# Another statically searched order of the same 3061 operations for a two-layer banded-attention and MLP kernel, with other engine choices for some of them

## The chip, the cores and the metric

The kernel runs on one core of a Trainium2 chip. A core has TensorE (PE in the profile, its weight loads PEld), VectorE (DVE), ScalarE (ACT), GpSimd (POOL) and SyncE (SP), which only issues transfers here. The metric is the device time of one execution in microseconds (us), as the median of the runs. A run more than 1.5% above the fastest of its kernel counts as slow, the others as fast.

## The reference, cut to what matters

```python
x = A_x                                                 # 2048 x 512, bf16
x = x + _A_ref(_layernorm(x), A_wqkv, A_wo)             # attention: 32 heads of 16, window of 256 back
x = x + _B_ref(_layernorm(x), B_w1, B_b1, B_w2, B_b2)   # MLP 512 -> 1792 -> 512, tanh GELU
x = x + _A_ref(_layernorm(x), A_wqkv, A_wo)             # the same weights a second time
x = x + _B_ref(_layernorm(x), B_w1, B_b1, B_w2, B_b2)
```

## The kernel before

The kernel first describes its work as nodes (engine, function, a nominal duration, what is read and written, PSUM banks taken and freed). Then three lists, found offline by a search, decide everything: `_ORDER` is the order in which nodes are put into the five engine queues, `_ALT` names the nodes that run on their second engine, and `_BANKS` is the PSUM bank of each allocation.

```python
for i in _ALT:                                  # second engine instead of the first
    nodes[i]["eng"], nodes[i]["fn"], nodes[i]["dur"] = nodes[i]["alts"][1][:3]
...
for i in _ORDER:
    ...                                         # asserts dependencies, takes and frees banks
return _ORDER
...
for i in order:                                 # an engine runs its own nodes strictly in this order
    nd = PL.nodes[i]
    S_.op(nd["eng"], ..., reads=phys(nd["reads"]), writes=phys(nd["writes"]), dma=nd["dma"])
```

Each engine works its queue in order and waits on semaphores for the others, so a node that is placed too early in a queue holds up everything behind it.

The unit of attention is a score visit: 512 score columns for four row groups on TensorE (`sc`), then two exponentials of 128x1024 on ScalarE, then one or two 0/1 masks, each on VectorE or GpSimd:

```python
add("pe", sc, 250.0, reads=rd, writes=["ps:" + gA, "ps:" + gB], ...)
for gi, g_ in enumerate((gA, gB)):
    add("act", ...activation(E[...], ps[...], AF.Exp, scale=SCALE)...)
for k, (n, off, cnt) in enumerate((HEADM if head else FULLM)[v]):
    n1 = cnt * w / 128.0
    add("dve", ...tensor_tensor(out=Ew, in0=Ew, in1=Mw, op=ALU.mult)..., 140.0 + 275.0 * n1,
        ..., alt=(("pool", ...same..., 100.0 + 1052.0 * n1, POOL_H, True),))
```

There are 150 visits and so 300 exponentials. Other nodes with two possible engines are the copies of Q and V out of PSUM (VectorE or ScalarE), the normalisation of the attention output and a small layernorm addition (both VectorE or GpSimd). The edited numbers 250, 140, 275, 100 and 1052 are nominal: no instruction that is issued depends on them.

The softmax here doesn't subtract the row's maximum and nothing guards it: scores larger than these inputs give would overflow.

Of the kernel before, what the change touches and what calls it, by code (L numbers as in the profile page):

```python
# [7 lines left out]
ALU = mybir.AluOpType  # L8
# [11 lines left out]
class _Sched:  # L20
# [148 lines left out]
    14, 7, 33, 8, 15, 34, 9, 16, 13, 35, 17, 36, 18, 4, 37, 0, 19, 10, 38, 1, 20, 2, 39, 45, 21, 3, 40, 22, 43, 23,  # L169
    41, 24, 25, 44, 42, 46, 91, 26, 47, 27, 28, 48, 89, 29, 30, 31, 52, 32, 92, 49, 90, 50, 93, 53, 94, 51, 11, 98,  # L170
    54, 99, 5, 6, 65, 95, 66, 67, 60, 61, 62, 63, 82, 96, 68, 97, 83, 84, 85, 144, 55, 56, 86, 57, 100, 58, 64, 69,
    111, 112, 75, 76, 77, 59, 113, 114, 78, 142, 162, 116, 143, 164, 145, 117, 115, 118, 146, 119, 147, 163, 12,
    148, 167, 120, 169, 70, 71, 72, 73, 215, 168, 106, 107, 149, 217, 108, 101, 79, 102, 150, 170, 103, 104, 216,
    74, 151, 121, 109, 122, 123, 124, 105, 128, 88, 125, 129, 130, 166, 131, 218, 110, 81, 219, 171, 132, 220, 172,
    221, 134, 245, 223, 173, 133, 181, 157, 224, 158, 183, 246, 175, 174, 247, 165, 182, 185, 222, 248, 187, 184,
    152, 153, 87, 154, 155, 249, 159, 135, 156, 252, 186, 253, 126, 160, 235, 254, 127, 161, 255, 188, 189, 236,
    237, 256, 80, 225, 238, 259, 138, 226, 258, 261, 227, 228, 136, 140, 137, 229, 260, 250, 263, 239, 141, 264,
    262, 176, 265, 267, 177, 268, 190, 266, 269, 271, 191, 273, 240, 192, 178, 272, 193, 275, 179, 241, 242, 277,
    274, 276, 284, 270, 243, 194, 286, 278, 230, 180, 231, 285, 244, 232, 288, 233, 287, 289, 195, 234, 196, 197,
    290, 198, 331, 292, 200, 199, 294, 201, 202, 203, 329, 349, 350, 293, 204, 300, 351, 291, 352, 483, 302, 353,  # L180
    301, 296, 295, 279, 298, 205, 297, 207, 373, 208, 206, 375, 209, 536, 210, 330, 537, 303, 374, 377, 211, 379,
    538, 212, 376, 280, 378, 381, 467, 539, 383, 281, 385, 299, 380, 387, 304, 332, 282, 333, 382, 213, 334, 283,
    386, 214, 384, 540, 389, 305, 257, 388, 359, 390, 360, 361, 306, 391, 335, 354, 307, 336, 355, 362, 308, 398,
    363, 366, 392, 251, 356, 400, 357, 367, 364, 358, 368, 369, 399, 314, 365, 315, 316, 317, 337, 370, 499, 318,
    309, 500, 371, 310, 311, 321, 804, 312, 338, 501, 313, 402, 322, 319, 393, 403, 502, 320, 652, 404, 653, 503,
    394, 505, 409, 410, 323, 339, 405, 340, 504, 507, 650, 341, 342, 509, 411, 416, 506, 417, 343, 556, 557, 508,
    558, 651, 418, 559, 541, 580, 401, 413, 788, 581, 414, 510, 582, 324, 654, 511, 583, 560, 415, 584, 512, 561,
    585, 562, 327, 563, 586, 564, 328, 588, 565, 406, 590, 407, 587, 420, 372, 344, 421, 408, 589, 422, 592, 325,
    345, 594, 346, 347, 655, 566, 567, 395, 326, 593, 348, 596, 568, 396, 569, 598, 423, 424, 139, 425, 597, 605,
    591, 573, 574, 544, 606, 595, 570, 607, 609, 542, 572, 575, 599, 576, 611, 437, 543, 438, 513, 439, 440, 397,  # L190
    427, 452, 514, 428, 429, 610, 453, 454, 577, 455, 442, 545, 462, 443, 444, 445, 515, 441, 463, 430, 612, 464,
    465, 600, 608, 466, 457, 516, 446, 517, 426, 518, 519, 458, 456, 459, 520, 521, 432, 412, 433, 434, 435, 601,
    447, 431, 460, 448, 449, 461, 436, 546, 526, 450, 547, 548, 451, 613, 527, 602, 419, 549, 603, 522, 615, 550,
    523, 524, 670, 525, 671, 672, 673, 528, 529, 614, 674, 617, 530, 531, 551, 552, 618, 553, 604, 484, 616, 619,
    621, 485, 532, 486, 623, 533, 487, 620, 554, 873, 488, 489, 622, 534, 694, 555, 490, 535, 491, 695, 492, 624,
    493, 494, 495, 696, 496, 698, 497, 700, 625, 498, 656, 699, 658, 657, 468, 626, 469, 701, 702, 470, 659, 704,
    471, 627, 703, 578, 472, 706, 628, 571, 727, 707, 473, 579, 474, 1011, 629, 475, 476, 708, 477, 478, 728, 479,
    729, 480, 719, 709, 481, 720, 660, 482, 730, 665, 731, 721, 820, 666, 732, 667, 741, 875, 668, 742, 710, 743,
    737, 711, 669, 661, 662, 738, 712, 663, 630, 664, 631, 632, 633, 713, 723, 634, 783, 725, 734, 640, 735, 635,
    636, 724, 876, 722, 637, 784, 638, 785, 786, 874, 639, 726, 758, 759, 787, 760, 761, 642, 744, 748, 749, 641,  # L200
    750, 736, 675, 751, 643, 745, 739, 762, 644, 768, 769, 697, 645, 770, 740, 771, 705, 676, 677, 678, 772, 778,
    779, 752, 780, 781, 877, 746, 763, 878, 764, 765, 646, 747, 753, 754, 755, 679, 766, 647, 680, 756, 767, 773,
    774, 757, 775, 776, 648, 681, 714, 1096, 777, 649, 782, 1098, 733, 836, 715, 687, 837, 688, 689, 682, 683, 716,
    789, 790, 684, 717, 690, 791, 691, 792, 685, 793, 794, 838, 1097, 795, 1099, 881, 693, 840, 1100, 879, 796,
    1101, 718, 842, 797, 880, 798, 799, 839, 800, 841, 801, 844, 882, 802, 898, 845, 803, 899, 900, 901, 692, 846,
    843, 902, 917, 686, 919, 847, 921, 923, 848, 918, 805, 922, 806, 920, 807, 808, 849, 809, 810, 811, 812, 925,
    850, 813, 851, 926, 883, 884, 885, 814, 924, 852, 927, 886, 929, 815, 887, 816, 931, 817, 818, 853, 819, 854,
    930, 855, 933, 856, 934, 888, 932, 857, 889, 890, 891, 935, 1116, 892, 942, 1117, 928, 944, 1118, 1119, 821,
    863, 822, 943, 823, 936, 824, 946, 825, 1120, 947, 937, 948, 858, 938, 859, 1059, 949, 860, 1060, 861, 826, 862,
    827, 828, 1061, 829, 864, 1063, 865, 893, 945, 894, 1065, 895, 896, 830, 897, 831, 1064, 1067, 832, 833, 1069,  # L210
    834, 1062, 1066, 903, 904, 835, 905, 1068, 906, 1140, 939, 1121, 907, 1142, 1122, 1123, 1070, 1124, 910, 911,
    1141, 866, 912, 867, 1125, 1144, 868, 913, 1145, 1071, 940, 914, 1146, 869, 915, 1143, 1148, 1072, 870, 957,
    1149, 958, 953, 871, 1150, 916, 1152, 954, 872, 1154, 1133, 1151, 955, 1134, 1135, 959, 1136, 1153, 960, 1073,
    961, 1137, 1156, 962, 1126, 1158, 1127, 1074, 1128, 1129, 950, 1157, 1130, 951, 1027, 1165, 952, 1132, 967,
    1167, 1104, 968, 1348, 1131, 981, 982, 969, 983, 1166, 984, 909, 1169, 1075, 996, 1105, 1155, 997, 1171, 1212,
    998, 999, 1006, 1007, 941, 1008, 1009, 1170, 991, 992, 1168, 993, 964, 1102, 994, 1210, 1172, 1103, 986, 987,
    995, 988, 1147, 965, 989, 976, 977, 1138, 1081, 1082, 1083, 908, 978, 1010, 1084, 979, 1076, 990, 1077, 966,
    1078, 963, 1079, 1213, 1159, 1001, 971, 1106, 980, 1107, 1080, 1108, 985, 972, 1109, 1085, 1002, 1000, 1003,
    1004, 1211, 973, 1086, 974, 1005, 1160, 956, 1087, 1110, 1088, 970, 1173, 1214, 1028, 1089, 975, 1161, 1090,
    1029, 1030, 1175, 1091, 1031, 1032, 1111, 1215, 1094, 1112, 1113, 1114, 1033, 1092, 1034, 1035, 1115, 1093,  # L220
    1036, 1174, 1037, 1177, 1038, 1039, 1179, 1095, 1176, 1012, 1013, 1040, 1041, 1178, 1014, 1042, 1181, 1015,
    1183, 1162, 1016, 1180, 1235, 1163, 1236, 1237, 1182, 1238, 1254, 1239, 1017, 1018, 1256, 1019, 1020, 1021,
    1216, 1022, 1255, 1184, 1023, 1258, 1433, 1024, 1260, 1025, 1185, 1434, 1026, 1259, 1218, 1364, 1164, 1219,
    1262, 1044, 1186, 1264, 1045, 1046, 1257, 1047, 1139, 1048, 1263, 1435, 1049, 1050, 1217, 1266, 1436, 1187,
    1051, 1268, 1052, 1188, 1053, 1054, 1055, 1267, 1301, 1043, 1270, 1189, 1302, 1272, 1269, 1056, 1304, 1057,
    1265, 1271, 1220, 1221, 1222, 1058, 1223, 1305, 1224, 1279, 1561, 1290, 1281, 1291, 1190, 1261, 1292, 1191,
    1280, 1192, 1193, 1303, 1313, 1314, 1315, 1306, 1316, 1283, 1194, 1323, 1284, 1324, 1437, 1297, 1273, 1200,
# [202 lines left out]
def bass_interleave_layers__sliding_block__dense_activation_gelu__prompt_kernel(  # L430
# [53 lines left out]
    ACT_H, POOL_H, DVE_H = 300.0, 60.0, 0.0  # L484
# [12 lines left out]
    with ExitStack() as kctx:  # L497
        S_ = _Sched(nc, kctx)

        def sb(name, shape, dtype=dt.bfloat16):  # L500
# [36 lines left out]
        add = PL.add  # L537
# [5 lines left out]
            reads=["ident"], writes=["ident"], prio=-200)  # L543
        add("pool", lambda e, B: e.affine_select(
            ident[:], ident[:], [[1, P]], ALU.is_ge, 0.0, base=0, channel_multiplier=-1), 300,
            reads=["ident"], writes=["ident"], prio=-200)
# [8 lines left out]
        for i, conds in enumerate((((1, HK, -1), (0, -HK, 1)), ((1, 0, -1),))):  # L555
            for st, base, cm in conds:
                add("pool", lambda e, B, i=i, st=st, base=base, cm=cm: e.affine_select(
                    mask01[:, i, :], mask01[:, i, :], [[st, HK]], ALU.is_ge, 0.0, base=base, channel_multiplier=cm), 250,
                    reads=["mask01"], writes=["mask01"], prio=50)
# [439 lines left out]
```

## Time and profile before

| | kernel before |
|---|---|
| time, median | 473.71 us when the prediction was made; 473.48 of 4 runs beside the changed kernel |
| span of the profiled run | 468.9 us |
| busy: TensorE, ScalarE, VectorE, GpSimd | 434.1, 388.6, 346.6, 203.5 us |
| first exponential starts, 64th ends | 15.47 us, 87.5 us |
| 300th exponential ends | 426.3 us |

The useful way to read this profile is by stage. The exponentials are good milestones, since every visit has two, both kernels have 300 of them in the same order of blocks, and ScalarE runs them in one line of the timeline. Between the 64th and the 65th ScalarE changes to GELU for the first time. The prediction shows the lines; the stretches after the first milestone are cut slightly differently here. The view is busy time by stretch (length, then each engine's busy us with its instructions in brackets, then TensorE's granted clock, 1.00 being full speed), for the kernel before:

```profile
15.40:54.10 38.70, 28.62 (x577) 16.96 (x573) 32.42 (x56) 32.43 (x38) 13.48 (x13) 0.91 0.30 81
54.10:87.50 33.40, 28.04 (x682) 18.11 (x683) 31.84 (x58) 31.00 (x36) 18.93 (x18) 0.90 0.32 79
87.50:148.60 61.10, 56.35 (x1139) 32.95 (x1136) 45.60 (x80) 54.02 (x66) 25.07 (x20) 1.00 0.19 41
148.60:426.30 277.70, 268.94 (x4827) 149.32 (x4826) 216.37 (x367) 252.81 (x299) 132.20 (x110) 1.00 0.16 32
```

They are exponentials 1 to 32, 33 to 64, 65 to 104 and 105 to 300. In the first two VectorE and ScalarE are both busy most of the time, and TensorE's granted clock is 0.91 and 0.90 instead of 1.

### The profile page before, as it was taken

Reading aid. Unit: us, or ns where it says so; the run is one execution under the profiler, and the core shown is the slowest. Engines: PE = TensorE matmul, PEld = TensorE weight load, DVE = VectorE, ACT = ScalarE, POOL = GpSimd, SP = SyncE. Lnnn points to the kernel's source line nnn. Section 1 sums busy time; section 2 is a strip of 40 time slices with the busy share of each in tenths; the row PEclk is TensorE's granted clock in tenths of the full one; section 3 lists DMA queues with packets and bytes.
Section 4 is the critical chain, followed back from the end, with each engine's and each line's share of the span. In section 5 each row is a group of like instructions: output and inputs, shape, how many; then the busy total and the mean of one; then the engine's idle time right before and its main releaser. Section 6 shows DMA issues by size and latency. Waiting matters only on the chain.

```text
span 468.9 us, 16891 instructions
## 1 busy us (share of the span) xinstructions
PE 434.1 (93%) x7627; PEld 245.0 (52%) x7627; DVE 346.6 (74%) x599; ACT 388.6 (83%) x469; POOL 203.5 (43%) x189
## 2 busy tenths in 40 slices
PE   8877698788989989999999999989999999899997
PEld 4543455544645545565556455545555544545453
DVE  4968999886867996758998786898857769933311
ACT  1588998997989889988899899889989989985441
POOL 4233447315455454644761166534349441434020
PEclk9997889999999999999999999999999999999999
DMA  8551031711120122101221201203020012020122
GB/s 247 202 133 53 15 68 24 194 29 39 25 48 4 36 51 29 31 2 31 43 59 35 51 1 30 45 14 66 1 59 19 3 27 62 3 58 1 30 73 67
DMA packets 47940, 23.51 MB, mean 50 GB/s; under 512 B 34172, under 2 KB 47356, under 8 KB 47868
## 3 DMA queue, kind: packets, MB, share of 16 engines
q1 hardware_dynamic: 47868, 22.43, 20.2%
q8 instruction: 60, 0.98, 0.9%
q14 instruction: 12, 0.10, 0.1%
HBM read 8.00 MB, written 2.10 MB: 22 GB/s over the span
## 4 chain that ended last, share of the span: by engine, by line
PE 74%; ACT 12%; DVE 10%; issue 2%; DMA 1%; POOL 0%; DVEq 0%; SPq 0%
PE ps L665 57%; ACT E L786 11%; PE ps L823 8%; PE ps L779 8%; DVE xn L635 2%; DVE KT L710 2%; DVE stat L612 1%; DVE E L795 1%; DMA X<-in_A_x_dram 1%; DMA xnTA<-xn 1%; DVE X L921 1%; DVE OD L833 1%; DVE QT L600 0%; DVE gT L897 0%; POOL rstd L622 0%
## 5 line engine op out<-in xcount | busy, mean ns | idle before, releaser
L786 ACT ACTIVATE E<-ps 128x1024 bf16<-128x1024 f32 x300 | 284.1, 1038 | 34.6 <-PE ps L779 33.8
L798 POOL TENSOR_TENSOR E<-E,mask 128x1024 bf16<-128x1024 bf16 (+3 forms) x65 | 109.9, 1697 | 89.3 <-ACT E L786 89.0
L665 PE MATMUL ps<-xnTB,W_sb 128*128 128x384 bf16 (+1 forms) x616 | 115.1, 322 | 4.6 <-issue 2.9
L665 PE MATMUL ps<-W_sb,gT 128*128 128x512 bf16 x448 | 112.2, 380 | 2.3 <-issue 2.3
L665 PEld LDWEIGHTS ps<-xnTB,W_sb 128*128 128x128 bf16 x616 | 57.1, 98 | 45.6 <-issue 5.2
L665 PE MATMUL ps<-xnTA,Wqkv_sb 128*128 128x256 bf16 x512 | 73.5, 278 | 3.2 <-DVE X L921 1.8
L779 PE MATMUL ps<-QT,KT 32*128 32x256 bf16 (+3 forms) x1920 | 62.1, 235 | 13.1 <-ACT E L786 7.4
L909 ACT ACTIVATE gT<-ps,b1T 128x384 bf16<-128x384 f32 (+1 forms) x100 | 50.7, 578 | 22.4 <-PE ps L665 22.2
L795 DVE TENSOR_TENSOR E<-E,mask 128x1024 bf16<-128x1024 bf16 (+3 forms) x91 | 61.0, 681 | 11.2 <-ACT E L786 10.9
L665 PEld LDWEIGHTS ps<-W_sb,gT 128*128 128x128 bf16 x448 | 40.4, 98 | 48.1 <-issue 8.0
L779 PEld LDWEIGHTS ps<-QT,KT 32*128 32x128 bf16 x1920 | 32.8, 93 | 60.9 <-ACT E L786 36.1
L665 PEld LDWEIGHTS ps<-xnTA,Wqkv_sb 128*128 128x128 bf16 x512 | 47.6, 99 | 22.0 <-issue 3.0
L841 POOL TENSOR_TENSOR Nb<-OD,Rc 128x512 bf16<-128x512 f32 x24 | 26.0, 1084 | 67.7 <-DVE Rc L837 67.7
L833 DVE STREAM_TRANSPOSE OD<-ps 128x1024 f32<-128x1024 f32 x32 | 39.8, 1244 | 20.4 <-PE ps L823 20.3
L917 POOL TENSOR_TENSOR Xb<-X,b2all 128x512 f32<-128x512 bf16 x32 | 38.0, 1194 | 29.6 <-DVE X L921 22.7
L823 PE MATMUL ps<-E,Va 64*17 64x64 bf16 (+3 forms) x1920 | 45.0, 234 | 3.6 <-ACT E L786 1.5
L921 DVE TENSOR_TENSOR X<-Xb,ps 128x512 bf16<-128x512 f32 x32 | 21.6, 683 | 34.7 <-PE ps L665 34.6
L823 PE MATMUL ps<-E,Vs 64*17 64x64 bf16 (+3 forms) x1920 | 45.4, 234 | 1.7 <-issue 1.7
L823 PEld LDWEIGHTS ps<-E,Va 64*17 64x17 bf16 x1920 | 39.2, 86 | 12.3 <-issue 8.0
L612 DVE BATCH_NORM_STATS2 stat<-X 128x6 f32<-128x512 bf16 x64 | 43.0, 682 | 3.0 <-DMA X<-in_A_x_dram 2.4
L897 DVE TENSOR_SCALAR gT<-ps,b1T 128x384 bf16<-128x384 f32 (+1 forms) x54 | 31.4, 591 | 13.2 <-PE ps L665 12.8
L710 DVE TENSOR_TENSOR KT<-ps,parmask 128x1024 bf16<-128x1024 f32 x32 | 38.7, 1210 | 3.3 <-PE ps L665 3.1
(49 smaller groups left out, 380.1 us busy)
## 6 DMA issues: line engine op xcount, KB each, us to landing
Vs<-Va SPq DMA_DIRECT2D x64, 68.0 KB, 2.1
W_sb<-in_B_w_dram SPq DMA_DIRECT2D x2, 1792.0 KB, 9.6
out_dram<-X SPq DMA_DIRECT2D x16, 128.0 KB, 1.8
X<-in_A_x_dram SPq DMA_DIRECT2D x3, 512.0 KB, 6.2
Wqkv_sb<-in_A_wqkv_dram SPq DMA_DIRECT2D x4, 256.0 KB, 5.2
X<-in_A_x_dram SPq DMA_DIRECT2D x2, 256.0 KB, 3.0
Wqkv_sb<-in_A_wqkv_dram SPq DMA_DIRECT2D x1, 512.0 KB, 6.3
Wo_sb<-in_A_wo_dram SPq DMA_DIRECT2D x1, 512.0 KB, 7.3
```

Of the source, the lines that this page charges most:

```text
L612: add("dve", lambda e, B, t=t, k6=k6: e.bn_stats(stat6[:, k6, :], X[:, t, :]), 680, reads=["X%d" % t], writes=["st%d" % k6], prio=prio[j], ...
L665: r = e.matmul(ps[:, B[g][0], cols], lhsT, rhs, start=st, stop=sp)
L710: add("dve", lambda e, B, g=g, i=i: e.tensor_tensor(out=KT[:, kb, 2 * i : 2 * i + 2, :, :].rearrange("p c m (a n) -> p (c m) a n", a=2), i ...
L779: x = e.matmul(ps[:, bk[r], o : o + n], KT[rows, kb, c, m, :], QT[rows, c, q : q + n], start=True, stop=True)
L786: add("act", lambda e, B, g_=g_, gi=gi: e.activation(E[:, 2 * gi : 2 * gi + 2, e0 : e0 + 512], ps[:, B[g_][0] : B[g_][0] + 2, :], AF.Exp, ...
L795: add("dve", lambda e, B, Ew=Ew, Mw=Mw: e.tensor_tensor(out=Ew, in0=Ew, in1=Mw, op=ALU.mult), 140.0 + 275.0 * n1, reads=["E%d_%d%s" % (sl, ...
L798: alt=(("pool", lambda e, B, Ew=Ew, Mw=Mw: e.tensor_tensor(out=Ew, in0=Ew, in1=Mw, op=ALU.mult), 100.0 + 1052.0 * n1, POOL_H, True),))
L823: x = e.matmul(ps[32 * r : 32 * r + VW, B[g][par], o * HK : (o + q_hi - q_lo) * HK], V[rows, (2 * b + m // 2) % VR, c * HC + 2 * r + par, ...
L833: add("dve", lambda e, B: e.transpose(OD[:, s, :], ps[:, B[g][0] : B[g][0] + 2, :]), 1245, reads=["ps:" + g], writes=["OD%d" % s], prio=pr ...
L897: add("dve", lambda e, B, g=g, fc=fc: e.tensor_scalar(out=gT[:, fc, 0:M], in0=ps[:, B[g][0], 0:M], scalar1=b1T[:, fc : fc + 1], scalar2=No ...
L909: add("act", lambda e, B, g=g, fc=fc: e.activation(gT[:, fc, 0:M], ps[:, B[g][0], 0:M], AF.Gelu_apprx_tanh, bias=b1T[:, fc : fc + 1], scal ...
L917: add("pool", lambda e, B, t=tau % T, xs=xs: e.tensor_tensor(out=Xb[:, xs, :], in0=X[:, t, :], in1=b2all[:], op=ALU.add), 1180, reads=["X% ...
```

## The change

The intent: the search that had found the three lists was continued, with other durations for the masks and the score visits. Apart from the three lists only nominal durations differ:

```diff
 _ORDER = [
-    14, 7, 33, 8, 15, 34, 9, 16, 13, 35, 17, 36, 18, 4, 37, 0, 19, 10, 38, 1, 20, 2, 39, 45, 21, 3, 40, 22, 43, 23,
+    14, 4, 33, 3, 13, 5, 15, 34, 16, 35, 0, 17, 36, 1, 18, 37, 2, 19, 7, 38, 20, 39, 21, 45, 40, 22, 23, 41, 43, 24,
  ... (all of _ORDER, _ALT and _BANKS is replaced)
-                add("pe", sc, 250.0, reads=rd,
+                add("pe", sc, 235.0, reads=rd,
  ...
-                    add("dve", ...tensor_tensor..., 140.0 + 275.0 * n1,
+                    add("dve", ...tensor_tensor..., 145.0 + 270.0 * n1,
  ...
-                        alt=(("pool", ...tensor_tensor..., 100.0 + 1052.0 * n1, POOL_H, True),))
+                        alt=(("pool", ...tensor_tensor..., 182.0 + 970.0 * n1, POOL_H, True),))
```

## The prediction

> **What bounds the kernel now.** I read the page first (shares and slices), then busy time in seven stretches that I cut at events of ScalarE's timeline, then the groups by shape, then the waits.
>
> ```profile
> PE 434.1 (93%) x7627; PEld 245.0 (52%) x7627; DVE 346.6 (74%) x599; ACT 388.6 (83%) x469; POOL 203.5 (43%) x189
> ...
> PE   8877698788989989999999999989999999899997
> ...
> DVE  4968999886867996758998786898857769933311
> ACT  1588998997989889988899899889989989985441
> ```
>
> TensorE looks like the bound (93%), but the slices say that the bound changes: up to slice 9 TensorE is at 6 to 8 tenths while VectorE and ScalarE stand at 8 or 9. So I cut the span at 15.4 us (first exponential starts), 44.9 us (ScalarE becomes dense), 87.5 us (64th exponential done, first GELU), 426.3 us (last exponential done).
>
> ```profile
> core 0: us, PE busy (x) PEld busy (x) DVE busy (x) ACT busy (x) POOL busy (x), PEclk, DMA share, GB/s
> 0.00:15.40 15.40, 13.47 (x87) 7.47 (x88) 9.02 (x22) 2.97 (x4) 4.74 (x19) 1.00 0.89 282
> 15.40:44.90 29.50, 22.13 (x369) 13.22 (x365) 23.39 (x37) 23.23 (x28) 10.02 (x10) 0.88 0.39 105
> 44.90:87.50 42.60, 34.53 (x892) 21.84 (x891) 40.87 (x77) 40.20 (x45) 22.39 (x22) 0.92 0.25 63
> 87.50:180.00 92.50, 85.30 (x1660) 48.86 (x1658) 73.89 (x127) 81.01 (x99) 41.57 (x34) 1.00 0.18 39
> 180.00:300.00 120.00, 119.82 (x2085) 67.73 (x2084) 94.73 (x164) 109.94 (x132) 59.17 (x52) 1.00 0.19 34
> 300.00:426.30 126.30, 120.16 (x2224) 65.67 (x2222) 93.34 (x156) 115.89 (x136) 56.53 (x45) 1.00 0.13 29
> 426.30:468.90 42.60, 38.70 (x326) 20.16 (x324) 11.31 (x19) 15.41 (x30) 9.09 (x10) 0.99 0.16 47
> ```
>
> Columns: length of the stretch, then each engine's busy us with instructions in brackets. Four regimes. (1) To 15.4 us: loads and the first layernorm. (2) 15.4 to 87.5: VectorE 64.3 of 72.1 us and ScalarE 63.4 of 72.1 are the bound together, TensorE has 15.4 us of holes. (3) 87.5 to 426.3: TensorE 325.3 of 338.8, 13.5 us of holes; ScalarE has 32.0 us of holes. (4) The last 42.6 us: MLP matmuls only.
>
> In regime 2 the holes of ScalarE lie at its start:
>
> ```profile
> 15.47 3.84 ACT L786 ACTIVATE E<-ps 128x1024 bf16<-128x1024 f32 x4 [1.88 <-PE ps L779]
> ...
> 23.87 4.69 ACT L786 ACTIVATE E<-ps 128x1024 bf16<-128x1024 f32 x5 [1.48 <-PE ps L779]
> ...
> 31.58 5.61 ACT L786 ACTIVATE E<-ps 128x1024 bf16<-128x1024 f32 x6 [1.12 <-PE ps L779]
> 39.05 5.61 ACT L786 ACTIVATE E<-ps 128x1024 bf16<-128x1024 f32 x6 [1.86 <-PE ps L779]
> ```
>
> (Start, length, instructions, idle time before.) Only 21 exponentials start in the first 29.4 us; with the few copies between them ScalarE is idle for about 6.3 us (29.5 minus 23.2). It waits for scores, and those wait for the VectorE copies and masked K tiles (1.21 us each) that feed them.
>
> **What the Trainium skill says.** "Perfetto Trace Analysis", section Identifying the Most-Contended Engine: matmul busy share is not a good measure of the distance to the limit because matmuls are pipelined. The trace agrees: a W2 matmul is shown with 380 ns, but 36 of them in a row took 7.93 us, 220 ns each. So "TensorE 100% busy" in regime 3 can hide bubbles and I don't take it as a floor. "SBUF — State Buffer", section Who interferes with whom: a VectorE instruction with two SBUF inputs and a GpSimd instruction that reads SBUF exclude each other, the later one fully blocks. The trace agrees: VectorE masks have a median of 675 ns but a longest of 2101 ns, about one GpSimd mask. "ScalarE: Activation LUTs", section What ACT_TABLE_LOAD costs: about 1283 ns for the load itself; here every one took 1283 ns, so switches matter if the new order has more of them.
>
> **The change part by part.** The program's 3061 operations, shapes and dependencies are the same. The four edited duration numbers never reach the chip; what does is the order of the queues, the choice of engine for some operations, and the PSUM banks. I counted each engine's queue in both kernels. Durations:
>
> ```profile
> L798 POOL TENSOR_TENSOR E<-E,mask 128x1024 bf16<-128x1024 bf16 x34 | 72.8, 2141 | 59.4 <-ACT E L786 59.3
> ...
> L795 DVE TENSOR_TENSOR E<-E,mask 128x1024 bf16<-128x1024 bf16 x50 | 37.9, 760 | 6.1 <-ACT E L786 6.1
> ```
>
> *ScalarE*: PSUM copies go from 22 to 14 (7 V copies and 1 Q copy go to VectorE) at some 0.61 us: 4.9 us less. Table loads: 19 switches in both, nothing. *VectorE*: +8 copies at 0.68 = +5.4; normalisations of the attention output 8 to 11 at 0.92 = +2.8; masks 91 to 81 (1 fewer of 256 columns at 0.26, 7 fewer of 512 at 0.58, 2 fewer of 1024 at 0.76) = -5.8. Sum +2.4 us, which is nothing where it has over 100 us of holes. *GpSimd*: 10 masks more (0.8 + 7 x 1.21 + 2 x 2.14 = 13.5), 3 normalisations fewer (-3.3): about +10 us on an engine at 43%. *TensorE*: the same matmuls; changes between row-tiled, column-tiled and full matmuls go from 325 to 330, nothing.
>
> So the total work doesn't decide; what lies in which regime does.
> *Regime 1.* In the new order TensorE has 8.2 us of matmul work ahead of the first score visit instead of 10.1 (256-column matmuls at 109 ns, 512 at 220): the four V matmuls that stood ahead of it now come after it. VectorE's first K tile comes before the second pair of tiles is normalised, in the old order after it and after a bn_stats of 0.69. My estimate: the first exponential at about 13.4 us instead of 15.5, 2 us earlier.
> *Regime 2.* VectorE's queue up to the 64th exponential: 6 masks fewer (4 x 0.76 + 0.58 + 0.26 = -3.9), 2 normalisations fewer (-1.8), one Q copy, one layernorm piece and three small ones fewer (-2.4), 4 V copies more (+2.7): 5.4 us less of a co-bound engine. ScalarE: 2 copies fewer, -1.2 us. GpSimd takes the 6 masks (+10.6 us with 4 long ones) where it has 39.7 us of holes. The ceiling of the gain is the 2 us plus ScalarE's holes, about 6.3 + 1.2; I expect regime 2 to end some 3.5 us earlier in all, since the slower GpSimd masks delay some attention products, and work moved out of the head (4 bias additions, a layernorm piece) comes back later.
> *Regime 3.* About 3.7 us less ScalarE work, but on the engine with 32 us of holes while TensorE is the bound; of the 13.5 us of holes of TensorE the better placing may close a little: 1 us.
> *Regime 4.* After the last score visit 112 W1 pieces, 8 output-projection matmuls and 90 W2 matmuls remain, against 112, 8 and 92: 2 x 0.22 = 0.4 us, taken as none because those two must run earlier.
> Sum: 3.5 + 1 = 4.5 us, 473.7 - 4.5 = 469.2.
>
> **Rivals.** (a) The head gains and nothing arrives: regime 3 is bound by TensorE and by its own chain, and starts when the first layer's last block is normalised, not at the 64th exponential. For it: TensorE's 100% from 180 to 300. Against it: a dense TensorE queue that starts earlier also ends earlier. It would give 472 to 474. (b) GpSimd's masks become the wait: each takes 2.14 us against 0.76, and 10 us more of it locks VectorE more often; the old order shows VectorE masks waiting up to 2.1 us. For it: the search counts a short VectorE mask at 415 ns, where the trace has 583, so it knows nothing of the lock. Against it: no row of the waits has TensorE waiting for a GpSimd mask. It would give 474 to 478. (c) The new order also closes most holes of ScalarE in the head and bubbles hidden inside TensorE's busy time, because it was searched with 235 ns for a score visit instead of 250. It would give 462 to 466. For it: 15.4 us of TensorE holes in regime 2. Against it: the orders of regime 3 look alike; TensorE work ahead of the 100th, 200th and 300th exponential differs by under 1 us.
>
> **Range and chances.** Executions of one kernel spread by 0.3%, 1.5 us; the head's gain I hold to 0 to 7 us, and regime 3 may go either way by 3 us. 80% range 464 to 473.5. Over 2% faster means under 464.2: rival (c), 0.11. Over 2% slower means over 483.2, for which nothing in the counts speaks: 0.01. Within 2%: 0.88.
>
> **What would show it.** First exponential near 13.4 us and the 64th done near 84 (was 87.5); VectorE's busy time until then about 5 us lower; ScalarE's total near 384; last exponential near 422, and from there again some 42.6 us. If the 64th exponential is early and the last one isn't, (a) holds. If VectorE masks take longer and TensorE's attention products wait for GpSimd, (b). If regime 3 shrinks by over 4 us, (c), and my belief that its order is as good as before was wrong.

## The result, and the profile after

The changed kernel takes 458.65 us (457.91 to 460.46, 4 runs), the kernel before 473.48 us (472.66 to 474.78, 4 runs). The ratio is 0.969, with a 95% interval of 0.9654 to 0.9726. Ratios are the mean time of one kernel's fast runs over that of the other's of the same rounds, so not quite the ratio of the medians quoted. The change is 3.1% faster; 469.2 was predicted, with a range down to 464.0. The gain is over three times the predicted one.

The page of the kernel after, its busy shares and slices:

```profile
PE 422.5 (93%) x7565; PEld 241.6 (53%) x7627; DVE 340.8 (75%) x600; ACT 385.4 (84%) x461; POOL 212.2 (47%) x196
...
PE   8986789989999999999989999998999998899997
...
DVE  6978899868878888977987669887666896725311
ACT  2899999989899998888788898998999899976250
```

The totals tell little: the shares are the same as before within a few per cent of the span. The slices tell where: ScalarE stands at 9 in slices 3 to 8, where the kernel before had 8, 8, 9, 9, 8, 9. Busy time by stretch, kernel after, cut at the same milestones (first exponential starts; 32nd, 64th, 104th and 300th ends):

```profile
0.00:12.50 12.50, 10.54 (x76) 6.38 (x78) 8.13 (x20) 3.08 (x4) 4.94 (x19) 1.00 0.86 255
12.50:44.90 32.40, 26.32 (x517) 16.30 (x522) 28.20 (x49) 31.67 (x36) 23.01 (x20) 1.00 0.58 171
44.90:78.10 33.20, 28.35 (x743) 17.81 (x747) 29.90 (x56) 30.61 (x34) 14.74 (x15) 0.95 0.31 60
78.10:135.30 57.20, 53.80 (x1125) 32.49 (x1133) 45.09 (x80) 53.75 (x66) 29.97 (x26) 1.00 0.18 33
135.30:412.80 277.50, 264.12 (x4783) 148.35 (x4824) 215.29 (x374) 250.53 (x294) 134.26 (x111) 1.00 0.18 32
412.80:456.20 43.40, 39.32 (x326) 20.32 (x326) 14.14 (x25) 15.82 (x29) 5.28 (x5) 0.99 0.15 43
```

Stage by stage, after minus before, in us:

| stage | before | after | difference |
|---|---|---|---|
| until the first exponential | 15.4 | 12.5 | -2.9 |
| exponentials 1 to 64 | 72.1 | 65.6 | -6.5 |
| exponentials 65 to 104 | 61.1 | 57.2 | -3.9 |
| exponentials 105 to 300 | 277.7 | 277.5 | -0.2 |
| after the last exponential | 42.6 | 43.4 | +0.8 |
| span | 468.9 | 456.2 | -12.7 |

These are one trace each; the medians differ by 14.8 us. So, as far as these traces go, the whole gain lies in the first third, and the 196 exponentials after it take the same time in both. In the second row ScalarE's busy time fell by 1.1 us only (63.43 to 62.28); its holes, length less busy time, fell from 8.7 to 3.3 us. The timeline of ScalarE in the new kernel (start, length, instructions, idle time before) shows it:

```profile
12.53 1.94 ACT L786 ACTIVATE E<-ps 128x1024 bf16<-128x1024 f32 x2 [0.64 <-PE ps L779]
...
15.14 1.94 ACT L786 ACTIVATE E<-ps 128x1024 bf16<-128x1024 f32 x2 [0.17 <-PE ps L779]
...
21.01 23.94 ACT L786 ACTIVATE E<-ps 128x1024 bf16<-128x1024 f32 x26 [0.34 <-PE ps L779]
```

The prediction shows four gaps of 1.1 to 1.9 us up to 39 us in the kernel before; here 26 exponentials run as one piece from 21.0 to 44.9 us, and at 45 us 32 are done instead of 22.

VectorE's groups by shape explain a part. The first two lines are of the kernel before until its 64th exponential, the next two of the kernel after until its own (busy us and mean ns of one, then idle time before):

```profile
L635 DVE TENSOR_SCALAR xn<-X,statmv,rstd 128x512 bf16<-128x512 bf16 x16 | 8.0, 504 | 1.4 <-POOL rstd L622 1.2
L795 DVE TENSOR_TENSOR E<-E,mask 128x512 bf16<-128x512 bf16 x7 | 4.1, 592 | 1.4 <-ACT E L786 1.4
```

```profile
L635 DVE TENSOR_SCALAR xn<-X,statmv,rstd 128x512 bf16<-128x512 bf16 x15 | 6.0, 418 | 0.4 <-DMA xnTB<-xn 0.2
L795 DVE TENSOR_TENSOR E<-E,mask 128x512 bf16<-128x512 bf16 x6 | 2.4, 419 | 0.0
```

The same instructions are shorter on average: a mask of 512 columns takes 419 ns instead of 592, a layernorm normalisation 418 instead of 504. With 6 to 16 of a kind, these means hang on a few long ones. Of the seven masks before, five took 413 to 427 ns, one 671 and one 1377. One normalisation took four times its usual time, while GpSimd was doing a mask of its own (19.40 to 21.04 us):

```profile
19.53 1.65 DVE L635 TENSOR_SCALAR xn<-X,statmv,rstd 128x512 bf16<-128x512 bf16 x1
```

VectorE masks of over 1 us number eleven in the kernel before, two of them in this stretch, and seven in the kernel after, none of them in this stretch; every one started while a GpSimd instruction was running. Over the whole kernel the masks did not all become shorter: 512 columns went from 583 to 513 ns, 1024 columns from 760 to 780. In this stretch GpSimd has more masks than before (it is busy for 42.7 us against 37.2), yet VectorE is held up less. VectorE's busy time until the 64th exponential is 66.2 us instead of 73.3.

### The profile page after: what moved, and what is told of

It is laid out like the page before. It is cut to its first block, busy times and chain, and to the rows that moved or that the text cites.

```text
span 456.2 us, 16825 instructions
## 1 busy us (share of the span) xinstructions
PE 422.5 (93%) x7565; PEld 241.6 (53%) x7627; DVE 340.8 (75%) x600; ACT 385.4 (84%) x461; POOL 212.2 (47%) x196
## 4 chain that ended last, share of the span: by engine, by line
PE 69%; ACT 21%; DVE 6%; issue 3%; DMA 2%; SPq 0%; DVEq 0%
PE ps L665 51%; ACT E L786 16%; PE ps L779 8%; PE ps L823 8%; ACT gT L909 2%; DVE OD L833 1%; PE ps L570 1%; ACT gT L900 1%; DVE E L795 1%; DMA xnTA<-xn 1%; DMA xnTB<-xn 1%; DVE gT L897 1%; DVE xn L635 1%; ACT L786 1%; ACT L909 1%
## 5 line engine op out<-in xcount | busy, mean ns | idle before, releaser
L786 ACT ACTIVATE E<-ps 128x1024 bf16<-128x1024 f32 x300 | 284.1, 1040 | 27.8 <-PE ps L779 27.1
L798 POOL TENSOR_TENSOR E<-E,mask 128x1024 bf16<-128x1024 bf16 (+3 forms) x75 | 122.7, 1648 | 82.1 <-ACT E L786 81.9
L665 PE MATMUL ps<-xnTB,W_sb 128*128 128x384 bf16 (+1 forms) x616 | 113.3, 322 | 5.1 <-DVE X L921 1.2
L665 PE MATMUL ps<-W_sb,gT 128*128 128x512 bf16 x418 | 108.7, 380 | 3.1 <-issue 2.1
L665 PE MATMUL ps<-xnTA,Wqkv_sb 128*128 128x256 bf16 x512 | 72.1, 274 | 3.2 <-ACT E L786 1.0
L779 PE MATMUL ps<-QT,KT 32*128 32x256 bf16 (+3 forms) x1920 | 61.4, 232 | 9.8 <-ACT E L786 6.2
L909 ACT ACTIVATE gT<-ps,b1T 128x384 bf16<-128x384 f32 (+1 forms) x100 | 51.2, 574 | 21.6 <-PE ps L665 21.3
L779 PEld LDWEIGHTS ps<-QT,KT 32*128 32x128 bf16 x1920 | 32.3, 93 | 56.7 <-ACT E L786 29.9
L795 DVE TENSOR_TENSOR E<-E,mask 128x1024 bf16<-128x1024 bf16 (+2 forms) x81 | 53.3, 670 | 10.0 <-ACT E L786 9.9
L823 PE MATMUL ps<-E,Vs 64*17 64x64 bf16 (+3 forms) x1920 | 44.4, 231 | 1.9 <-issue 1.9
L823 PE MATMUL ps<-E,Va 64*17 64x64 bf16 (+3 forms) x1920 | 44.0, 231 | 2.0 <-issue 1.0
L622 POOL TENSOR_TENSOR rstd<-rstd,mhalf 128x2 f32<-128x2 f32 x32 | 23.5, 734 | 34.5 <-DVE rstd L618 33.0
## 6 DMA issues: line engine op xcount, KB each, us to landing
W_sb<-in_B_w_dram SPq DMA_DIRECT2D x2, 1792.0 KB, 11.7
```

The source lines that it names most:

```text
L665: r = e.matmul(ps[:, B[g][0], cols], lhsT, rhs, start=st, stop=sp)
L779: x = e.matmul(ps[:, bk[r], o : o + n], KT[rows, kb, c, m, :], QT[rows, c, q : q + n], start=True, stop=True)
L786: add("act", lambda e, B, g_=g_, gi=gi: e.activation(E[:, 2 * gi : 2 * gi + 2, e0 : e0 + 512], ps[:, B[g_][0] : B[g_][0] + 2, :], AF.Exp, ...
L795: add("dve", lambda e, B, Ew=Ew, Mw=Mw: e.tensor_tensor(out=Ew, in0=Ew, in1=Mw, op=ALU.mult), 145.0 + 270.0 * n1, reads=["E%d_%d%s" % (sl, ...
L798: alt=(("pool", lambda e, B, Ew=Ew, Mw=Mw: e.tensor_tensor(out=Ew, in0=Ew, in1=Mw, op=ALU.mult), 182.0 + 970.0 * n1, POOL_H, True),))
L823: x = e.matmul(ps[32 * r : 32 * r + VW, B[g][par], o * HK : (o + q_hi - q_lo) * HK], V[rows, (2 * b + m // 2) % VR, c * HC + 2 * r + par, ...
```

## The experiments

Most of them splice the two kernels: nodes, dependencies and data are identical, so one can take the new queues up to the n-th exponential and the old ones for all that is left (or the reverse). At such a cut the two kernels have done nearly the same set of nodes, and the few that differ simply follow in the order of the second kernel. PSUM banks are kept where they are free and otherwise chosen anew. Every splice gave correct results. Milestones below are the ends of exponentials in ScalarE's timeline of the profiled run (a merged row divided evenly), in us. They are of one trace each: the same old queues took between 277.7 and 280.5 us for exponentials 105 to 300 in different runs, so a difference of 2 us or less late in the kernel says little.

| kernel | median | ratio to before | 12th | 32nd | 64th | 104th | 300th | span |
|---|---|---|---|---|---|---|---|---|
| before | 473.5 | 1 | 33.4 | 54.1 | 87.5 | 148.6 | 426.3 | 468.9 |
| after | 458.65 | 0.969 | 26.5 | 45.0 | 78.1 | 135.3 | 412.8 | 456.2 |
| head12 | 469.34 | 0.989 | 27.3 | 50.5 | 85.6 | 146.6 | 424.9 | 466.7 |
| head32 | 468.60 | 0.992 | 27.7 | 46.1 | 86.6 | 146.7 | 425.8 | 468.1 |
| head32b | 465.14 | 0.987 | 27.0 | 45.4 | 82.0 | 142.4 | 421.1 | 463.4 |
| head66 | 464.13 | 0.983 | 26.3 | 44.8 | 78.2 | 139.8 | 420.1 | 462.4 |
| head110 | 461.88 | 0.981 | 26.9 | 45.3 | 78.9 | 138.0 | 417.5 | 460.0 |
| rest110 | 474.46 | 1.003 | 33.9 | 55.3 | 89.1 | 150.5 | 427.5 | 470.9 |
| order_only | 477.86 | 1.012 | 29.1 | 49.7 | 82.8 | 143.4 | 428.7 | 472.6 |
| engines_only | 483.97 | 1.021 | 32.3 | 51.2 | 91.6 | 152.5 | 438.0 | 480.3 |
| masks_old | 470.33 | 0.996 | 26.6 | 46.6 | 79.9 | 140.7 | 424.8 | 468.2 |
| copies_old | 465.02 | 0.982 | 28.8 | 48.3 | 82.9 | 140.4 | 418.7 | 462.1 |
| multi | 468.28 | 0.992 | 27.6 | 46.0 | 79.4 | 136.9 | 421.9 | 465.4 |
| warm | 483.64 | 1.021 | 34.0 | 54.8 | 97.5 | 158.0 | 438.5 | 480.7 |

The kernel before had a median of 473.18, 473.33 and 474.32 us beside the three sets of experiments.

### head32

```diff
-_ORDER = old
+_ORDER = new up to the 32nd exponential, then what is left in the old order
-_ALT = old
+_ALT = new for the nodes of that head, old for the others
```

> The new queues up to the 32nd exponential, then the old order and the old engine choices (11 operations differ at the seam). Theory H (the gain is made at the very start, where ScalarE had holes; there the new trace is 10 exponentials ahead at 45 us): 32nd exponential done near 45 us, then the old pace, 462 to 466 us, 8 to 11 us under the kernel before. Rival M (the gain is spread over all stages or comes from the engine choices of the whole kernel): 469 to 473 us.

Measured: 468.60 us, ratio 0.992. Neither theory: the 32nd exponential comes 8.0 us early, the 64th only 0.9. The lead was lost right behind the seam, and the waits of this kernel between 46 and 60 us name the reason (who waited, for whom, us in total, times, longest):

```profile
POOL Xb L895 <- DMA b2all<-in_B_b_dram: 6.7, 1, 6.7
...
DVE xn L613 <- POOL rstd L600: 5.7, 1, 5.7
```

The load of the bias b2 had been issued behind the 1.8 MB load of W2, because the new queues issue W2 early and the old ones b2. The old GpSimd queue had a bias addition next, which waited 6.7 us for it; the layernorm power behind it, VectorE's normalisation behind that and TensorE in turn all stood still. So this run doesn't decide between the theories: it shows what a single early node in an in-order queue costs.

### head32b

```diff
 head of the order, as in head32
-... W2 ...
+... X12, b2all, W2 ...
```

> head32 again with its seam mended: there the load of b2 stood behind the 1.8 MB load of W2, and GpSimd's bias addition waited 6.7 us for it and held up everything after it. Here X12 and b2 are issued before W2. If that wait ate the lead: the lead of 9 to 10 us at the 32nd exponential stays at 7 us or more at the 64th, and the time is 461 to 465 us. If the lead falls to under 3 us at the 64th even so, the start alone doesn't carry the gain, and the time stays at 467 to 470 us.

Measured: 465.14 us, ratio 0.987. The lead is 8.7 us at the 32nd exponential and 5.5 at the 64th, between the two marks set; the time lies at the edge of the first. The start carries more than half of the gain (8.2 of 14.8 us), and the 32 exponentials after it, in the old queues, lose 3 us of the lead. How much of that is the seam was not separated.

### head12

```diff
+_ORDER = new up to the 12th exponential, then old; _ALT likewise
```

> The new queues up to the 12th exponential only, the old ones after it (28 operations differ at the seam). The new trace is 6.9 us ahead there. If the lead, once made, stays whatever follows: 7 us ahead at the 64th too, 465 to 467.5 us. If VectorE's backlog takes it back (the old queues do the skipped VectorE work before the next exponentials): under 4 us ahead at the 32nd and 469 to 473 us.

Measured: 469.34 us, ratio 0.989. The lead of 6.1 us at the 12th exponential shrinks to 3.6 at the 32nd and 1.9 at the 64th. The second case holds: a lead made by running scores earlier alone is taken back. The 28 operations that differ at this seam all lie on one side: the old order has done them by the 12th exponential, and the new one has not. VectorE's busy time until the 64th exponential is 72.2 us here, close to the 73.3 of the kernel before and far from the 66.2 of the kernel after. That the unrelieved VectorE is the reason fits this number but isn't isolated by it.

### head66

```diff
+_ORDER = new up to the 66th exponential, then old; _ALT likewise
```

> The new queues up to the 66th exponential (14 operations differ at the seam), the old ones after it. The new trace is 9.4 us ahead at the 64th exponential and 13.2 us ahead at the 104th. If the 4 us between come of the new queues of that stretch: 9 to 10 us ahead at both, 462.5 to 465.5 us. If they are given by the head start alone (less work left over): 13 us ahead at the 104th, 459 to 462 us as with the cut at 110.

Measured: 464.13 us, ratio 0.983, in the first range set. The lead is 9.3 us at the 64th exponential and 8.8 at the 104th. So the further gain of stage 65 to 104 was not given by the head start alone.

### head110

```diff
+_ORDER = new up to the 110th exponential, then old; _ALT likewise
```

> The new queues up to the 110th exponential (past the second GELU phase), the old ones after it (6 operations differ at the seam). H: the lead of 12.7 us that the new trace has at its second GELU phase stays to the end: 459 to 462.5 us. M: about a third of the gain, 467 to 470 us.

Measured: 461.88 us, ratio 0.981, 11.3 us of the 14.8. The time is in the range of theory H. The profiled run had a spell of lower clock in stage 65 to 104 (0.97 there, as head66 had, against 1.00 in the kernel after), which is why it is 10.6 us ahead at the 104th exponential and not 13.3. At this equal clock the stage took 59.1 us here and 61.6 in head66: the new queues of the stage are worth 2.5 us. At full clock, the traces have 57.2 to 57.5 us with the new queues (after, copies_old, multi) and 60.0 to 61.4 with the old ones (before, head12, head32, head32b, rest110, warm).

### rest110

```diff
+_ORDER = old up to the 110th exponential, then new; _ALT likewise
```

> The reverse: the old queues up to the 110th exponential, the new ones after it. H: 470 to 473.5 us, at most 3 us of gain. M: two thirds of the gain, 462 to 465 us.

Measured: 474.46 us, ratio 1.003 (interval 1.0009 to 1.0057). The new queues from the 110th exponential on gain nothing, which is even less than H expected (470 to 473.5). From the 104th to the 300th exponential the times are 277.7 (before), 277.5 (after), 277.0 (rest110), 279.5 (head110) and 280.3 us (head66). The old rest behind a new head looks some 2 us slower than in its own place, but warm, which has the old queues throughout, took 280.5 us there. So why head110 lacks 3 us of the gain stays open.

### order_only

```diff
 _ORDER, _BANKS: new
-_ALT = new
+_ALT = old
```

> The new order and PSUM banks, but every operation on the engine on which the old kernel had it. If the order carries the gain: 458 to 462 us. If the choice of engines does (fewer copies on ScalarE, masks on GpSimd): 466 to 473 us.

Measured: 477.86 us, ratio 1.012. Neither mark: the new order with the old engine choices is 19 us slower than the changed kernel and slower than the kernel before. It loses 4.7 us against the kernel after up to the 64th exponential and 11.2 us more from there to the 300th.

### engines_only

```diff
 _ORDER, _BANKS: old
-_ALT = old
+_ALT = new
```

> The old order and banks with the engine choices of the new kernel. If the choice is good by itself: 468 to 472 us. If a choice fits only the order that it was searched with, as order_only says: 476 to 490 us.

Measured: 483.97 us, ratio 1.021. The other way round is worse still, in the second range set. Together with order_only this is the clearest result:

| | old engine choices | new engine choices |
|---|---|---|
| old order | 473.5 us | 484.0 us |
| new order | 477.9 us | 458.65 us |

Each part alone loses 4 to 10 us, both together gain 15. The bank list goes with the order here, and its own share was not tried. So in this kernel the new order pays only with the engine choices that it was searched with. This holds for the whole and not for every stage: order_only is 4.7 us ahead of the kernel before at the 64th exponential, and engines_only 2.9 us ahead at the 32nd, before it falls behind. Both lose in exponentials 105 to 300, which take 285.4 and 285.5 us.

### masks_old and copies_old

```diff
 new kernel, but in _ALT
+  masks_old:  the masks as in the old kernel (60 change sides)
+  copies_old: the copies of Q and V out of PSUM as in the old kernel (18 change sides)
```

> The new kernel with the masks alone (VectorE or GpSimd) on the engine of the old one; 60 masks change sides, 10 net. If the masks' side is what makes order_only 19 us slower than the new kernel: 470 to 478 us, with most of the loss after the 104th exponential. If it is the copies on ScalarE and the other pieces: 458 to 463 us.

Measured: 470.33 us, 11.7 more than the changed kernel. The loss is 1.8 us at the 64th exponential, 5.4 at the 104th and 12.0 at the 300th. It is spread over the kernel as expected, at the lower edge of the time. Exponentials 65 to 104 take 60.7 us here (60.6 in order_only, 60.9 in engines_only), as in the old queues, and 57.5 in copies_old. So nearly the whole gain of that stage needs the new order and the new side of the masks together.

> The new kernel with the copies of Q and V out of PSUM on the engine of the old one (8 more on ScalarE net, 18 change sides). masks_old lost 11.7 us to the new kernel, order_only 19.2; if the losses add up, this loses the rest less what the normalisations and small pieces lose: 462 to 466 us. If a copy costs only its own time (8 x 0.61 us at most): 458.5 to 463 us.

Measured: 465.02 us, within the first mark: 6.4 more than the changed kernel, for 8 more copies of 0.61 us on ScalarE (4.9 us at most). The loss comes early: 2.3 us at the 12th exponential, 4.8 at the 64th, 5.1 at the 104th, 5.9 at the 300th. Half of the 9.4 us that the new kernel is ahead at the 64th exponential therefore hang on the copies' engine, and 1.8 us on the masks'. The two losses, 11.7 and 6.4, add up to 18.1 of order_only's 19.2 us. VectorE's busy time until the 64th exponential is 65.5 us here, less than the 66.2 of the changed kernel, and ScalarE's from the first exponential on is 1.7 us more; the rest of the 4.8 us is a start that is 0.6 us later and more holes of ScalarE (5.8 us against 3.3). So a lighter VectorE does not by itself make the head faster.

### warm

```diff
-                    for c, kb, m, q, o, n in pieces:
+                    for c, kb, m, q, o, n in pieces * (2 if b in (1, 2, 3) else 1):
```

> The kernel before with every score visit of the blocks 1 to 3 computed twice (same result, some 0.21 us more TensorE work for each of 30 visits, 6 us in all), so that TensorE has shorter pauses in the head, where the old trace has 13.7 us at half clock. If the lower clock costs what the runs of one kernel suggest (2.8 us for each 0.01 of mean clock) and the extra work fits into TensorE's holes: clock 0.995 or more, 470 to 473 us. If the clock there costs nothing: 473.5 to 480 us at a higher clock.

Measured: 483.64 us, ratio 1.021, at a mean clock of 0.98. A miss on both counts. The clock didn't rise, and stage 33 to 64 took 42.7 us instead of 33.4, while TensorE's busy time in it rose by 4.6 us only (32.6 against 28.0). The waits of ScalarE in that stage, first warm, then the kernel before:

```profile
ACT E L786 <- PE ps L779: 10.7, 8, 2.6
```

```profile
ACT E L786 <- PE ps L779: 1.9, 2, 1.6
```

So TensorE, which has holes there, still lies on the path of that stage: extra work ahead of the scores costs more than its own time. The granted clock of the stage was 0.88 against 0.90, three spells of 3.4 us at half clock instead of one of 6.8, so a part of the loss can be that. How much of the head's gain is due to the lower clock could not be isolated in this way.

The runs themselves give an estimate of the clock's share. The first 34 fast runs of the kernel before beside the experiments had mean clocks of 0.982 to 0.996: those at 0.982 took 474.1 us (mean of 4), at 0.989 472.8 (13), at 0.996 471.2 (3). A straight line through all 34 gives 1.7 us for each 0.01 (the 2.8 in the expectation had six slow runs in it), and 1.4 through all 82 fast runs of the three sets, with a wide scatter. At equal clock the changed kernel is 12 to 13 us faster: 458.4 (mean of 2) against 471.2 at 0.996, 460.5 (1 run) against 472.8 at 0.989. It also runs at a higher clock on the whole, and 1 to 2 us of the 14.8 go with that. Whether the clock is a cause or follows from shorter pauses of TensorE stays open.

Kept traces with the same queues but other clocks bound it stage by stage. One more spell of 3.4 us at half clock went with 0.8 us in exponentials 1 to 32 (rest110 against before), with 0.1 to 0.4 us in 33 to 64 (head110 against head66, multi and after), and with some 1.7 us in 65 to 104 (head110 against after and multi). The kernel before has two such spells more than the kernel after in the first of these stages and one more in the second. An estimate from these numbers is 2 x 0.8 + 0.4 = 2 us of the 9.4 us gained at the 64th exponential; by it, most of the head's gain is not the clock.

### multi

```diff
+_ORDER = new to the 140th exponential, old to the 210th, then new; _ALT likewise
```

> New queues to the 140th exponential, old ones to the 210th, new ones again after it. In the two traces the old kernel took 98.5 us from the 140th region to the 204th exponential where the new one took 99.8, 1 to 3 us more depending on the cut. If stages are independent: 455.5 to 458 us, faster than both. If the seams cost more than they give: 458.5 to 462 us.

Measured: 468.28 us, ratio 0.992. Neither mark was met. The old queues were a little faster between the 124th and the 204th exponential (127.9 us against 129.9), but the cut fell inside a stage and the seam cost far more: exponentials 125 to 144 took 36.4 us instead of 30.1. No version beat the changed kernel.

## Why the prediction was wrong

The direction was right and the size was not. By its own steps:

*The bound by stages* held in part. In the head VectorE and ScalarE are the busiest, but TensorE lies on the path too (warm), and less work on VectorE did not help by itself (copies_old). The last 196 exponentials took 277.7 and 277.5 us, as predicted. That TensorE alone bounds them was too simple: with the same matmuls and only the masks' side changed they took 284.1 us (masks_old).

*Regime 1*: 2 us were predicted, 2.9 measured (first exponential from 15.47 to 12.53 us, predicted 13.4). Right in kind.

*Regime 2* is the step that failed: "I expect regime 2 to end some 3.5 us earlier in all". It ended 9.4 us earlier. The counts beside it were right: ScalarE's work 1.15 us less (1.2 predicted), VectorE's 7.0 us less (5.4 counted; much of the rest is the shorter time of single instructions). What failed is the term for the waits: 3.5 us leaves 0.3 for closed holes after the 2 us of the start and the 1.2 of ScalarE's work, and 5.35 us of holes were closed (2.9 + 1.15 + 5.35 = 9.4). A ceiling was written down, "the 2 us plus ScalarE's holes, about 6.3 + 1.2", which makes 9.5. That the gain meets it so closely is luck: it counted only the holes of the first 29.4 us, where the regime has 8.7 us of them, of which 3.3 remain, and the start gave 2.9 instead of 2. I took about a third of it, on a guess that slower masks on GpSimd and postponed work would give it back. They didn't: masks_old says that the masks' side in the head is worth 1.8 us in favour of the new choice, and copies_old that the Q and V copies, whose V part I had counted as a mere exchange (0.61 us here for 0.68 there), are worth 4.8 us. Why their place closes these holes was not followed wait by wait.

*Regime 3*: 1 us predicted, 4.1 measured, of which 3.9 in its first stage. "A little" was wrong there and right for the rest: ScalarE's holes in exponentials 65 to 104 fell from 7.1 to 3.45 us. head110 against head66 shows that the queues of this stage do 2.5 us of it or more, and masks_old that the masks' side is a necessary part.

*Regime 4*: none predicted, 0.8 us worse measured.

*Rivals.* (a), that nothing of the head's gain arrives, is refuted: head66 and head110 keep 6 and 9 us of it to the 300th exponential. (b) is refuted for this order: the head's masks became shorter, although GpSimd did more, and TensorE waits for no GpSimd mask. (In the kernel before it does once, for 0.3 us, where the prediction had no such row.) Both signs of (b) appear when the new order gets the old engine choices: VectorE masks of 512 columns average 634 ns in order_only and 644 in masks_old, against 513 in the changed kernel, and TensorE's weight loads wait 3.2 and 2.9 us in all for GpSimd masks. Those runs have fewer masks on GpSimd, not more, and how much of their loss this makes was not separated. (c) was the nearest, though 458.65 lies below its 462 to 466 too; that the 235 ns of the search are the reason was not tested. It was given 0.11, and its "against", that the orders of regime 3 look alike, compared sums of TensorE work to within 1 us, which says nothing of how that work is spread between the visits. That counting also could not see what order_only and engines_only show: a sum over a queue is blind to whether order and engine fit. (The duration numbers edited are five, not the four of the prediction; nothing rests on it.)

## What to carry to other kernels

When a schedule's totals hardly change, add up the holes of the engine that bounds the stage and treat that sum as a live possibility, not as a ceiling to be discounted: here the search closed holes and removed next to no work. An order and an engine assignment were one decision here: each alone lost 4 to 10 us and both together gained 15, so don't carry over half of a searched schedule without measuring it. Cutting two schedules at a milestone and splicing them is a cheap way to find which stage a gain comes from, as long as the seam is looked at in the trace first.

## What the Trainium skill lacked or had wrong

- "SBUF — State Buffer", section Who interferes with whom: that a VectorE instruction with two SBUF inputs and a reading GpSimd instruction exclude each other agrees with the longest masks (2101 ns before, 2077 after). So does its statement that issue order decides who blocks: all masks of over 1 us started while a GpSimd instruction was running. What it lacks is the price in a mixed stream: in the head a 512-column mask took 592 ns on average in one order and 419 ns in the other, with more GpSimd work in the second. So the busy time of GpSimd did not predict the loss here.
- "TensorE: Matmul & The Clock Gate", sections What's actually happening and HAM oscillation: they tie the return to the low clock to an idle window of some 3.4 us. In the head of the kernel before, the clock fell to half twice without one: it fell after 3.4 us in which TensorE was busy for 1.05 us (34.35 to 37.76 us of the span, longest pause 1.72 us) and after 3.4 us in which it was busy for 0.99 us (51.41 to 54.82, a pause of 1.3 us and one of 1.4 that reaches past the fall). Each spell then lasted some 6.8 us, although TensorE was busy for 88% and 85% of it. So a mostly idle window was enough here. The page's section on a second failure mode does tell of short pauses between bursts that bring the low clock; what it lacks is a number for them.
- "Perfetto Trace Analysis", section Identifying the Most-Contended Engine: it ranks the engines once, for the whole kernel. By busy time that is TensorE (93%), by the weight-load share that the page prefers for TensorE (53%) it is ScalarE (84%); neither ranking names a stage. The part after the 104th exponential gained 0.2 us, and the largest gain was in a stage where ScalarE was busy for 88% of its length and VectorE for 89%. Its next section does speak of several regimes, and the cut by milestones is how that was found here.
- No page of it that I read says what extra work on an engine with holes can cost when it lies ahead of the bound one: stage 33 to 64 of warm became 9.3 us longer with 4.6 us more of TensorE's busy time, at nearly the same clock.
